# Pacing the first 24 loads of a transformer-block kernel by the landings of earlier loads

## Chip, cores and metric

The kernel runs on one core of one Trainium2 chip. The metric is device time in microseconds (us): the median of several executions. A profile's "span" is from the first to the last instruction of the profiled execution and is about 2 us shorter than the device time. Runs are compared only where they are of the same state ("fast"). A run is called slow when it is over 1.5% above the fastest run of the same kernel.

## The reference

A diffusion-transformer block with 2 batches of 256 tokens, width D = 1152, 2 heads and an MLP of 4608, in bf16. `c` gives six modulation vectors.

```python
mod = (silu(c) @ w_mod).reshape(B, 6, 1, D)      # w_mod: D x 6D
shift_a, scale_a, gate_a, shift_m, scale_m, gate_m = ...
h   = layernorm(x) * (1 + scale_a) + shift_a
q, k, v = split(h @ wqkv)                        # wqkv: D x 3D
a   = softmax(q k^T * Dh**-0.5) v @ wo
x   = x + gate_a * a
h2  = layernorm(x) * (1 + scale_m) + shift_m
out = x + gate_m * (gelu(h2 @ w_fc1) @ w_fc2)
```

The weights are 50 MB. Each byte is read once, so the kernel is a race between 50 MB of loads and the matmuls.

## The kernel before

All large loads go through one helper, on SyncE's queue, in program order. Each load has a completion semaphore. SyncE waits only where a load overwrites a buffer that is still in use.

```python
def dma(dst, src, nbytes, name, is_out=False, eng="sp", run=4096):
    eff = 1.0 if run >= 4096 else (1.08 if run >= 2304 else (1.15 if run >= 1536 else (1.3 if run >= 1024 else 1.42)))
    return S.op(eng, 500.0 if eng == "sp" else 150.0, lambda e: e.dma_start(dst, src), reads=[src], writes=[dst],
                name=name, dma_bytes=nbytes * eff, is_out=is_out)
```

`dma_bytes` is weighted: among these loads, those in short runs count up to 1.3 times their bytes. The first loads are issued in this order; I number them from 1:

```python
for b in range(2): dma(X[...], xv[b], ..., "ld_x%d" % b)                     # 1-2, 576 KB each
for (ka, kb) in ((0, KC), (KC, KT)):                                        # KC = 5, KT = 9
    for k0 in range(0, KT, 3): dma(WSC[...], wmod_v[...], ...)              # 3-5: 480 KB; 11-13: 384 KB (scale_a)
    for kt in range(ka, kb):   dma(WK[:, kt, :], wqkv_v[:, kt, D:2 * D], ..) # 6-10 and 14-17: 288 KB (K weights)
for k0 in range(0, KT, 3):     dma(WSH[...], wmod_v[:, k0:k0 + 3, 0:D], ...)  # 18-20: 864 KB (shift_a)
# ... cut ...
for kt in range(KT): dma(WQ[:, kt, :], wqkv_v[:, kt, 0:D], ...)              # 21-29: 288 KB; reuses WSC's space
dma(WV, ...)                                                               # 2592 KB
for k0 in range(0, KT, 3): dma(WMODR[:, k0:k0 + 3, :], wmod_v[:, k0:k0 + 3, 2 * D:6 * D], ...)  # 3 x 3456 KB
dma(WO, ...)                                                               # 2592 KB, then w_fc1, w_fc2
```

PE's order, as far as it matters: dummy matmuls to warm up; the three parts of the first w_mod product (`sca`, 128x2 outputs, loads 3 to 5), between transposes of the normalized x; K weight by weight; the second scale product; the shift product; Q; attention with V; then `rows()`, the row-modulation product of `c` with 4608 columns of w_mod. Its last third needs the third 3456 KB load, called **the last large w_mod load** from here on. Then come Wo and the MLP.

Of the kernel before, what the change touches and what calls it, by code (L numbers as in the profile page):

```python
# [544 lines left out]
def build_kernel(nc, x, c, wqkv, wo, w_mod, w_fc1, w_fc2, out):  # L545
    S = Sched()
# [4 lines left out]
    with (  # L551
# [104 lines left out]
        wfc1_v = w_fc1.rearrange("(k p) f -> p k f", p=P)  # L656
        wfc2_v = w_fc2.rearrange("(k p) f -> p k f", p=P)

        def dma(dst, src, nbytes, name, is_out=False, eng="sp", run=4096):
            eff = 1.0 if run >= 4096 else (1.08 if run >= 2304 else (1.15 if run >= 1536 else (1.3 if run >= 1024 else 1.42)))  # L660
            return S.op(eng, 500.0 if eng == "sp" else 150.0, lambda e: e.dma_start(dst, src), reads=[src], writes=[dst],  # L661
                        name=name, dma_bytes=nbytes * eff, is_out=is_out)

        def dve(cost, fn, reads, writes, name):
            return S.op("dve", cost, fn, reads=reads, writes=writes, name=name)
# [18 lines left out]


        dma(CSB[0:18, :], c.rearrange("b (k p) -> (b k) p", p=P), 18 * 256, "ld_c", eng="act")
        for b in range(2):
            dma(X[:, 2 * b:2 * b + 2, :], xv[b], 2 * P * D * 2, "ld_x%d" % b)
        for (ka, kb) in ((0, KC), (KC, KT)):
            w = (kb - ka) * P  # L690
            for k0 in range(0, KT, 3):
                dma(WSC[:, k0:k0 + 3, ka * P:kb * P], wmod_v[:, k0:k0 + 3, D + ka * P:D + kb * P], 3 * P * w * 2,
                    "ld_sc%d_%d" % (ka, k0), run=w * 2)
            for kt in range(ka, kb):
                dma(WK[:, kt, :], wqkv_v[:, kt, D:2 * D], P * D * 2, "ld_wk%d" % kt, run=2304)
# [3 lines left out]
        def wfc1_load(q):  # L699
# [5 lines left out]
             reads=[ONES], writes=[IDENT], name="ident")  # L705
# [176 lines left out]
        for kt in range(KT):  # L882
            for b in range(2):
                src, dst = HK[:, kt, b * 256:(b + 1) * 256], HX[:, kt, b * 256:(b + 1) * 256]
# [271 lines left out]
def bass_standalone__dit_block__diffusion_kernel(  # L1156
    nc: bass.Bass,
    x: bass.AP,
    c: bass.AP,
    wqkv: bass.AP,  # L1160
    wo: bass.AP,
    w_mod: bass.AP,
    w_fc1: bass.AP,
    w_fc2: bass.AP,
    out: bass.AP,
):
    build_kernel(nc, x, c, wqkv, wo, w_mod, w_fc1, w_fc2, out)
# [28 lines left out]
```

## Time and profile before

| | before |
|---|---|
| device time, median | 250.9 us (249.12 to 251.25) |
| span of the profile | 246.9 us |
| PE busy | 240.9 us, 98% |
| third part of the first w_mod product: load landed, PE began | 10.55, 10.59 us |
| first K weight landed, PE began K | 11.50, 11.90 us |
| last large w_mod load landed, PE needed it | 68.71, 69.90 us |

From the profile page of the kernel before: the head line, busy time by engine, and of the 40 equal slices (6.2 us each) PE, the granted TensorE clock, the DMA engines' busy share, all in tenths, and the bytes moved.

```profile
span 246.9 us, 4129 instructions
PE 240.9 (98%) x1814; PEld 149.5 (61%) x1823; DVE 69.9 (28%) x179; ACT 63.8 (26%) x129; POOL 19.6 (8%) x33
...
PE   7799999999999999999999999999999999999995
...
PEclk9999999999999999999999999999999999999999
DMA  6999999999999999999944560000000000000000
GB/s 245 348 378 393 391 315 411 420 425 424 408 387 341 310 365 391 393 390 383 357 137 158 191 191 3 0 0 0 3 16 16 16 19 16 16 19 16 22 28 18
```

PE never pauses after the second slice, and DMA is saturated for half of the span. The chain of waits that ended last, in order of time (start us, us, what), shows where the two meet: one load at the start, and PE alone from then on.

```profile
2.70 7.85 DMA arena<-in_w_mod_dram
10.55 0.05 issue
10.59 0.67 PE psum L680 x15
...
11.90 1.92 PE psum L680 x16
```

The table of stretches, before (columns: stretch; length; PE, weight loads, VectorE, ScalarE, GpSimd with instruction counts; granted clock, DMA share, GB/s):

```profile
0.00:12.00 12.00, 9.21 (x81) 4.62 (x82) 6.68 (x22) 7.47 (x12) 3.17 (x11) 1.00 0.84 294
12.00:24.00 12.00, 12.00 (x145) 10.63 (x145) 4.84 (x18) 2.29 (x5) 0.00 (x0) 1.00 1.06 385
24.00:36.00 12.00, 11.92 (x154) 9.19 (x153) 5.39 (x17) 5.37 (x11) 0.00 (x0) 1.00 0.99 351
36.00:48.00 12.00, 11.95 (x58) 5.66 (x58) 2.22 (x4) 1.87 (x4) 0.00 (x0) 1.00 1.04 414
```

SyncE's own waits before contain no load (the only DMA wait, of 1.1 us, is for an output store at the very end):

```profile
SPq L661 <- PE psum L680: 109.2, 21, 23.1
SPq L661 <- DVE arena L1140: 96.4, 13, 37.7
SPq L485 <- DMA out_dram<-arena: 1.1, 1, 1.1
```

So it issues loads far ahead: load 5 waits 7.85 us from issue to landing, mostly in the queue behind others.

### The profile page before, as it was taken

To read this page: it belongs to the slowest core of one execution; us is meant where nothing else is said; L and a number is where in the kernel's file an instruction comes from. 1 tells how busy PE (TensorE), PEld (TensorE's weight loads), DVE (VectorE), ACT (ScalarE), POOL (GpSimd) and SP (SyncE) were. 2 spreads that over 40 slices of the span, in tenths; PEclk is the share of its full clock that TensorE was granted. 3 is DMA by queue.
4 is the path that set the end of the run, shared out by engine and by line. 5 is a ranking of instruction groups with operands and counts; after the bars stand their busy time and mean duration, and the time that the engine had idled before them with its cause. 6 is when DMAs were issued, how large, how long until landed. Compare 5 with 4: busy or idle time off the path is not lost.

```text
span 246.9 us, 4129 instructions
## 1 busy us (share of the span) xinstructions
PE 240.9 (98%) x1814; PEld 149.5 (61%) x1823; DVE 69.9 (28%) x179; ACT 63.8 (26%) x129; POOL 19.6 (8%) x33
## 2 busy tenths in 40 slices
PE   7799999999999999999999999999999999999995
PEld 2589954566656766798544444444566666666675
DVE  3742440555322678950000000000011222211112
ACT  5630340344301404984233222333000000000000
POOL 1300000000012167500000000000000000000000
PEclk9999999999999999999999999999999999999999
DMA  6999999999999999999944560000000000000000
GB/s 245 348 378 393 391 315 411 420 425 424 408 387 341 310 365 391 393 390 383 357 137 158 191 191 3 0 0 0 3 16 16 16 19 16 16 19 16 22 28 18
DMA packets 27644, 51.59 MB, mean 209 GB/s; under 512 B 1511, under 2 KB 15591, under 8 KB 26475
## 3 DMA queue, kind: packets, MB, share of 16 engines
q1 hardware_dynamic: 27216, 50.14, 56.1%
q0 software_dynamic: 384, 1.19, 1.5%
q8 instruction: 14, 0.23, 0.4%
q14 instruction: 3, 0.02, 0.0%
q10 hardware_dynamic: 27, 0.00, 0.0%
HBM read 50.14 MB, written 1.19 MB: 208 GB/s over the span
## 4 chain that ended last, share of the span: by engine, by line
PE 93%; DMA 3%; ACT 1%; SPq 1%; issue 0%; DVE 0%
PE psum L680 91%; DMA arena<-in_w_mod_dram 3%; PE psum L683 2%; ACT arena L1049 1%; SPq L661 1%; ACT arena L1033 1%; DVE arena L785 0%; DVE arena L1139 0%; DVE arena L1140 0%; DVE arena L776 0%
## 5 line engine op out<-in xcount | busy, mean ns | idle before, releaser
L680 PE MATMUL psum<-arena 128*128 128x384 bf16 (+7 forms) x1707 | 237.1, 305 | 3.3 <-POOL arena L703 1.4
L680 PEld LDWEIGHTS psum<-arena 128*128 128x128 bf16 (+1 forms) x1716 | 143.7, 97 | 92.0 <-issue 3.9
L1139 DVE TENSOR_TENSOR arena<-psum,arena 128x384 f32<-128x384 f32 (+3 forms) x14 | 7.0, 501 | 119.1 <-PE psum L680 119.1
L1059 ACT ACTIVATE arena<-psum 128x512 bf16<-128x512 f32 (+1 forms) x44 | 22.5, 522 | 42.6 <-PE psum L680 42.6
L675 ACT ACTIVATE arena<-psum 128x512 bf16<-128x512 f32 (+7 forms) x29 | 15.4, 553 | 36.2 <-PE psum L680 33.8
L677 DVE CAST arena<-psum 128x512 bf16<-128x512 f32 (+4 forms) x23 | 14.0, 621 | 32.1 <-PE psum L680 32.0
L1028 POOL TENSOR_TENSOR arena<-arena 128x384 f32<-128x384 f32 x12 | 10.9, 912 | 11.1 <-DVE arena L1027 9.9
L724 DVE BATCH_NORM_STATS2 arena<-arena 128x6 f32<-128x384 f32 (+1 forms) x18 | 9.5, 548 | 1.1 <-DMA arena<-in_x_dram 1.0
L683 PEld LDWEIGHTS psum<-arena 128*128 128x128 bf16 (+2 forms) x107 | 6.4, 97 | 2.6 <-DMA arena<-in_c_dram 0.8
L683 PE MATMUL psum<-arena 128*128 128x128 bf16 (+2 forms) x107 | 7.8, 209 | 0.1
L1033 ACT ACTIVATE arena<-arena 128x1152 bf16<-128x1152 f32 x4 | 5.4, 1353 | 9.5 <-DVE arena L1032 9.5
L1027 DVE TENSOR_TENSOR arena<-psum,arena 128x384 f32<-128x384 f32 x12 | 6.6, 548 | 3.2 <-PE psum L680 3.0
L1140 DVE TENSOR_TENSOR arena<-arena 128x384 bf16<-128x384 f32 (+3 forms) x14 | 7.0, 501 | 0.5
L1049 ACT ACTIVATE arena<-psum,arena 128x128 bf16<-128x128 bf16 x16 | 6.1, 460 | 3.2 <-PE psum L683 2.5
L661 POOL DMA_DIRECT2D dit_scratch<-arena x2 | 1.3, 629 | 61.6 <-DVE arena L677 61.6
L1046 DVE TENSOR_SCALAR arena<-psum,arena 128x128 bf16<-128x128 bf16 x20 | 5.5, 336 | 2.0 <-PE psum L683 1.8
L924 ACT ACTIVATE arena<-psum,arena 128x256 bf16<-128x256 f32 x8 | 3.7, 470 | 6.9 <-PE psum L680 5.4
L728 POOL TENSOR_TENSOR arena<-arena 128x1 f32<-128x1 f32 x6 | 3.3, 552 | 8.3 <-DVE arena L727 8.3
L887 ACT ACTIVATE arena<-arena 128x256 bf16<-128x256 bf16 x6 | 2.5, 495 | 4.3 <-DVE arena L881 4.3
L920 DVE TENSOR_REDUCE arena<-psum 128x2 f32<-128x512 f32 x4 | 2.8, 689 | 1.5 <-PE psum L680 1.5
L785 DVE TENSOR_SCALAR arena<-psum,arena 128x256 bf16<-128x256 bf16 x7 | 2.4, 349 | 2.7 <-PE psum L683 1.4
L928 DVE TENSOR_TENSOR arena<-arena 128x512 bf16<-128x512 bf16 x4 | 2.8, 688 | 0.1
(37 smaller groups left out, 30.9 us busy)
## 6 DMA issues: line engine op xcount, KB each, us to landing
arena<-in_w_mod_dram SPq DMA_DIRECT2D x3, 3456.0 KB, 26.3
arena<-in_w_fc_dram SPq DMA_DIRECT2D x9, 1152.0 KB, 7.9
arena<-in_w_fc_dram SPq DMA_DIRECT2D x4, 2592.0 KB, 20.4
arena<-in_wqkv_dram SPq DMA_DIRECT2D x18, 288.0 KB, 10.4
arena<-in_w_mod_dram SPq DMA_DIRECT2D x3, 864.0 KB, 12.1
arena<-in_wqkv_dram SPq DMA_DIRECT2D x1, 2592.0 KB, 10.2
arena<-in_wo_dram SPq DMA_DIRECT2D x1, 2592.0 KB, 39.7
arena<-in_w_mod_dram SPq DMA_DIRECT2D x3, 480.0 KB, 7.1
```

The source lines that it names most:

```text
L675: act(c_act(n), lambda e: e.activation(out=dst, in_=src, func=ACTF.Copy), [src], [dst], name)
L677: dve(c_dve_psum16(n) if psum16 else c_dve_psum32(n), lambda e: e.tensor_copy(dst, src), [src], [dst], name)
L680: S.instr(lambda e: e.matmul(o, lhsT=l, rhs=r, start=st, stop=sp, **kw), reads=[l, r], writes=[o])
L683: S.instr(lambda e: e.transpose(o, i_, idn), reads=[i_, idn], writes=[o])
L724: dve(550, lambda e, s=s, o=o: e.bn_stats(out=o, in_=s), [s], [o], "bn_%s_%d" % (tag, ci))
L1027: dve(550, lambda e, o=o, ga=ga, x1c=x1c: e.tensor_tensor(out=x1c, in0=o, in1=ga, op=ALU.mult), [o, ga], [x1c], "wo_t1_%d_%d" % (t, ci))
L1028: S.op("pool", 930, lambda e, xs=xs, x1c=x1c: e.tensor_tensor(out=x1c, in0=x1c, in1=xs, op=ALU.add), reads=[x1c, xs], writes=[x1c], name=" ...
L1033: act(1344, lambda e: e.activation(out=xn2, in_=x1, func=ACTF.Identity, scale=rs, bias=nm), [x1, rs, nm], [xn2], "xn2_%d" % t)
L1049: act(440, lambda e, o=o, dst=dst, s1=s1, s2=s2: e.activation(out=dst, in_=o, func=ACTF.Identity, scale=s1, bias=s2), [o, s1, s2], [dst], ...
L1059: act(c_act(ntok), lambda e: e.activation(out=dst, in_=o, func=ACTF.Gelu_apprx_tanh), [o], [dst], "gelu_%d_%d" % (f, tok0))
L1139: dve(c_dve_psum32(w), lambda e, o=o, gm=gm, t1=t1: e.tensor_tensor(out=t1, in0=o, in1=gm, op=ALU.mult), [o, gm], [t1], "fc2_t1_%d_%d" % ( ...
L1140: dve(c_dve_32(w), lambda e, t1=t1, x1c=x1c, ost=ost: e.tensor_tensor(out=ost, in0=t1, in1=x1c, op=ALU.add), [t1, x1c], [ost], "fc2_out_%d ...
```

## The change

The intent: no load should compete with an earlier one that PE needs sooner. Each of the first 24 loads waits until the load about 1.2 MB (weighted) ahead of it has landed. Nothing else changes; the order of instructions on every engine is the same.

```diff
+        flight = []
+
         def dma(dst, src, nbytes, name, is_out=False, eng="sp", run=4096):
             eff = ...
-            return S.op(eng, ...)
+            u = S.op(eng, ...)
+            if eng == "sp" and not is_out and len(flight) < 24:
+                ahead = 0
+                for v in reversed(flight):
+                    ahead += v.dma_bytes
+                    if ahead > 1.2e6:
+                        u.instrs[0].deps.add(v.instrs[0])
+                        break
+                flight.append(u)
+            return u
```

More of the change, by code (lines that the diff above doesn't have):

```diff
@@ L657, in build_kernel @@
         wfc2_v = w_fc2.rearrange("(k p) f -> p k f", p=P)
+        flight = []
         def dma(dst, src, nbytes, name, is_out=False, eng="sp", run=4096):
             eff = 1.0 if run >= 4096 else (1.08 if run >= 2304 else (1.15 if run >= 1536 else (1.3 if run >= 1024 else 1.42)))
-            return S.op(eng, 500.0 if eng == "sp" else 150.0, lambda e: e.dma_start(dst, src), reads=[src], writes=[dst],
-                        name=name, dma_bytes=nbytes * eff, is_out=is_out)
+            u = S.op(eng, 500.0 if eng == "sp" else 150.0, lambda e: e.dma_start(dst, src), reads=[src], writes=[dst],
+                     name=name, dma_bytes=nbytes * eff, is_out=is_out)
+            if eng == "sp" and not is_out and len(flight) < 24:
[7 more added lines that the diff above has]
+            return u
         def dve(cost, fn, reads, writes, name):
```

## The prediction

> **What bounds the kernel now.** The page: PE 98% busy in a span of 246.9 us, and the chain of waits is PE for 93%. The only other large piece is a DMA wait of 7.85 us at the start: the third of the first three w_mod loads, issued at 2.70, landed at 10.55 us. PE idles 0.6 us for it and 0.8 us for the VectorE step behind it (timeline). After 11.9 us PE has no gap over 0.25 us. So better loading gains only in the first 12 us: VectorE is busy with layernorm until 10.57 us and did that step at 11.29, so at most about 0.7 us (0.3%).
>
> **What the change does.** The order of instructions is the same on all engines; SyncE alone gets waits on landings among the first 24 loads. Intended: no later load competes with the one PE needs next. There is little to win: by 9.75 us the DMA engines had moved about 2.66 MB, and x plus the three w_mod loads are 2.65 MB.
>
> **What it costs.** An isolated load (the last three w_fc1 loads, 1152 KB) takes 5.6 us from issue to landing; its packets (1024 bytes, 46 ns each on 16 engines) take 3.3 us of it: about 2.3 us fixed, my estimate. [...] A paced load has this covered only if about 0.7 to 0.85 MB are still queued when its wait ends. The rule leaves less in places (estimates):
> - second w_mod load: 0.49 MB left, bubble 0.7 us
> - first K weight: 0.5 us; two or three others 0.1 to 0.25 us
> - second Q weight: it waits for the last shift load with one 0.29 MB load behind that: 1.3 us.
>
> Total about 2.6 us of lost DMA time.
>
> **What lies on the critical path.** (a) The third w_mod load lands 0.3 to 0.5 us later (about 11.0), and PE's K stage with it. (b) The DMA queue is backlogged from 2 to 69 us, so lost time is not recovered. The last large w_mod load (4608 columns) lands at 68.71 and PE needs it at 69.9: 1.2 us of slack. Landing 2.6 us later, it stalls PE in the row-modulation stage: total shift 2.6 - 1.2 = 1.4 us, which contains (a). Loads after it have more slack (Wo 8.7 us, first w_fc1 24 us).
>
> **Prediction.** 250.9 + 1.4 = 252.3 us; range 250.3 to 254.3. Faster by over 2%: 0.005; within 2%: 0.965; slower by over 2%: 0.03.
>
> **What would show it.** SyncE's waits gain rows ending with DMA landings. GB/s falls in the first two slices and near 30 us. The third w_mod load lands near 11.0 us. SyncE issues the Q weights at 28 to 35 us, not 19 to 25. The chain of waits shows a DMA piece from in_w_mod near 70 us, about 1 us long. PE busy time and granted clock stay.
>
> **What would make it wrong.** A load alone may be quicker (less queueing): then the bubbles halve and the effect is under 0.5 us. If different DMA engines are slow at different times, pacing adds up the slowest of each load: a loss of 4 us, 253.5. If PE idles longer before 12 us its clock may drop (the skill's "TensorE: Matmul & The Clock Gate", Part 1, gives a window of about 3.4 us; this trace has the first 5.7 us of matmuls at half rate, 427 ns for 512 columns): 1.5 us more.

## The result, and the profile after

The changed kernel took 260.02 us in the median of 4 fast runs (257.56 to 260.88) against 250.95 us. The ratio is 1.0376, with a 95% interval of 1.0309 to 1.0444: slower. (The ratios are taken from fast runs alone; they are not quite the ratios of the medians, which here would give 1.0361.) The predicted 252.3 us, with its range of 250.3 to 254.3, was wrong.

The profile page, after, the same lines:

```profile
span 255.5 us, 4140 instructions
PE 243.7 (95%) x1823; PEld 150.6 (59%) x1823; DVE 69.9 (27%) x179; ACT 63.8 (25%) x129; POOL 19.6 (8%) x33
...
PE   6679999999987999999999999999999999999995
...
PEclk9959999999999999999999999999999999999999
DMA  6798969999999999999995334000000000000000
GB/s 246 227 293 248 302 203 345 406 425 420 421 419 389 353 368 363 393 392 378 392 332 182 105 111 169 0 0 0 0 18 15 15 18 15 15 18 15 15 29 21
```

Slices 2 to 6 of the GB/s line lost between a fifth and over a third. The clock fell to half in the third slice, and PE has a new gap in slices 12 and 13. The chain after:

```profile
1.23 4.62 DMA arena<-in_x_dram
5.84 0.02 issue
5.86 4.33 DMA arena<-in_w_mod_dram
10.18 0.02 issue
10.20 3.98 DMA arena<-in_wqkv_dram
14.18 0.14 issue
14.31 3.57 PE psum L691 x16
...
36.33 4.32 DMA arena<-in_wqkv_dram
...
44.90 33.52 DMA arena<-in_w_mod_dram
78.42 0.04 issue
78.47 6.13 PE psum L691 x63
```

Loads now hang on loads: x, a w_mod part, a K weight, each issued at the landing of another. The last large w_mod load lands at 78.42 us (68.71 before), and PE starts on it at 78.47. From there on PE waits for no load. 78.47 - 69.90 = 8.57 us, and the spans differ by 255.5 - 246.9 = 8.6 us: the whole loss has arisen by that point.

SyncE's waits after, where the loads have come in:

```profile
SPq L663 <- DMA arena<-in_w_mod_dram: 9.0, 6, 2.1
SPq L663 <- DMA arena<-in_wqkv_dram: 8.3, 6, 4.2
SPq L474 <- DMA arena<-in_w_mod_dram: 5.9, 2, 4.2
SPq L663 <- DMA arena<-in_x_dram: 3.7, 1, 3.7
```

The table of stretches after:

```profile
0.00:12.00 12.00, 7.90 (x65) 3.76 (x65) 6.01 (x19) 7.47 (x12) 3.17 (x11) 1.00 0.72 230
12.00:24.00 12.00, 10.23 (x103) 8.15 (x104) 3.69 (x11) 2.29 (x5) 0.00 (x0) 0.72 0.88 273
24.00:36.00 12.00, 12.00 (x165) 10.95 (x163) 4.59 (x13) 2.39 (x4) 0.00 (x0) 1.00 0.83 274
36.00:48.00 12.00, 11.61 (x87) 5.63 (x84) 2.62 (x13) 2.98 (x7) 0.00 (x0) 1.00 0.92 327
```

The last column times 12 us gives the bytes by 48 us: (294 + 385 + 351 + 414) x 12 = 17.3 MB before, (230 + 273 + 274 + 327) x 12 = 13.2 MB after. The missing 4.1 MB, at the 414 GB/s of the last stretch before, are 9.9 us of DMA time. The landings say the same: load 24 (the fourth Q weight) landed 42.07 - 32.31 = 9.8 us later, and the last large w_mod load 9.7 us later. Nothing of the loss is recovered on the way, and none is added after load 24.

How the lateness grew, from the trace's record of landings (us):

| load | before | after | late by |
|---|---|---|---|
| 5, third w_mod part | 10.55 | 11.98 | 1.4 |
| 6, first K weight | 11.50 | 14.18 | 2.7 |
| 10, fifth K weight | 14.86 | 17.36 | 2.5 |
| 13, last of the second w_mod part | 18.12 | 21.78 | 3.7 |
| 17, last K weight | 21.52 | 27.36 | 5.8 |
| 20, last shift load | 29.30 | 36.27 | 7.0 |
| 24, fourth Q weight | 32.31 | 42.07 | 9.8 |
| last large w_mod load | 68.71 | 78.42 | 9.7 |

### The profile page after: what moved, and what is told of

The parts are those of the page before. It is cut to its first block, busy times and chain, and to the rows that moved or that the text cites. A ratio compares the mean times of both kernels' runs of the same rounds, so it can differ in the third digit from the quotient of the medians.

```text
span 255.5 us, 4140 instructions
## 1 busy us (share of the span) xinstructions
PE 243.7 (95%) x1823; PEld 150.6 (59%) x1823; DVE 69.9 (27%) x179; ACT 63.8 (25%) x129; POOL 19.6 (8%) x33
## 4 chain that ended last, share of the span: by engine, by line
PE 76%; DMA 20%; SPq 2%; ACT 1%; issue 0%; DVE 0%
PE psum L691 74%; DMA arena<-in_w_mod_dram 15%; DMA arena<-in_wqkv_dram 3%; DMA arena<-in_x_dram 2%; SPq L663 2%; PE psum L694 2%; ACT arena L1060 1%; ACT arena L1044 1%; DVE arena L1150 0%; DVE arena L1151 0%
## 5 line engine op out<-in xcount | busy, mean ns | idle before, releaser
L1039 POOL TENSOR_TENSOR arena<-arena 128x384 f32<-128x384 f32 x12 | 10.9, 912 | 11.1 <-DVE arena L1038 10.0
L794 ACT ACTIVATE arena<-psum,arena 128x256 bf16<-128x256 bf16 x3 | 1.3, 472 | 9.7 <-PE psum L691 6.5
```

The source lines that it names most:

```text
L1039: S.op("pool", 930, lambda e, xs=xs, x1c=x1c: e.tensor_tensor(out=x1c, in0=x1c, in1=xs, op=ALU.add), reads=[x1c, xs], writes=[x1c], name=" ...
```

## The experiments

All outputs are right. The theories:

- **A.** What counts is the DMA time lost by load 24. It passes unchanged to the last large w_mod load, and the 1.2 us of slack there are subtracted. Whatever PE loses before it only shortens its wait for it.
- **B.** PE's separate stalls add up, each a loss by itself.
- **C.** The early part (late K, clock at half) is the cause.

On why so much DMA time was lost: the **simple model** of the prediction (one server with a fixed cost per load), and **S**: a landing is that of the slowest of 16 DMA engines, and the fast ones run dry meanwhile. The Trainium skill ("DMA: Bandwidth & Descriptors", "Why a DMA increments its semaphore by 16 and not by 1") says that a DMA runs on up to 16 engines that finish independently. The trace agrees: in the changed kernel the 16 increments of one of the first 24 loads lie 0.5 to 2.6 us apart. Pacing is not what spreads them: in the kernel before it is 0.4 to 2.8 us, and in e11, which loses nothing, 0.6 to 2.9. There the DMA share stayed at 0.99 to 1.06 from 12 to 36 us (before), so the fast engines were not idle but went on with later loads.

e1 to e8 ran on one chip, e9 to e12 on another.

### e1: only the late part paced

```diff
-                    if ahead > 1.2e6:
+                    if ahead > 1.2e6 and len(flight) >= 10:
```

> Loads 1 to 10 (x, first w_mod, K weights 0 to 4) are free, only loads 11 to 24 are paced. In the changed kernel the landings ran late against before by 2.5 us after load 10 and by 9.7 us at load 24, and the last 4608-column w_mod load landed 9.7 us late against 1.2 us of slack. Theory A (what counts is the DMA time lost before that load, less its slack): about 9.7 - 2.5 = 7.2 us late there, so the kernel is 7.2 - 1.2 = 6.0 us slower than before, with the clock at full speed and K starting near 11.9 us. Rival B (PE's stalls add up: 4.9 us early, 0.7 and 3.0 us later): taking the early pacing away takes away the 4.9 us, so 3.7 us slower. Rival C (what costs is the cold TensorE clock and the late K stage): under 1 us slower.

Measured: 256.93 us median of 4. Two runs (256.53, 253.43) are fast, two (257.33, 258.57) slow, at clocks of 0.98 to 0.99 in all four. The ratio of the fast ones is 1.0198 (1.0092 to 1.0304), so 5.0 us, with two runs only. C is out: the late part alone costs most of the loss. A and B are both within the interval. In its profile (a slow run, so only for the order of events) PE began on the last large w_mod load at 76.96 us, at that load's landing of 76.92. Here, after a stall of about 3 us at that load, the clock record shows half speed from 77.7 to 81.1 us, which lengthens this run after the load as well.

### e2: only the early part paced

```diff
-            if eng == "sp" and not is_out and len(flight) < 24:
+            if eng == "sp" and not is_out and len(flight) < 10:
```

> Only loads 1 to 10 are paced. PE's start of K is late as in the changed kernel (K began at 14.3 instead of 11.9 us, and half the clock until about 19.7), about 4.9 us by the second part of the w_mod product. Theory A: DMA is only about 2.5 us late at the last 4608-column w_mod load, and PE comes to it 4.9 us late, so no stall there: 4.9 us slower than before, all of it before 24 us. Rival C (early part is everything): 8 to 9 us slower. Rival B: 4.9 us. So with e1: A has 6.0 + 4.9 more than the 8.6 us of the whole, B has 3.7 + 4.9 = 8.6.

Measured: 252.93 us against 249.79; ratio 1.0123 (1.0067 to 1.018), 3.1 us, less than the 4.9 expected. In its profile the last large w_mod load landed 3.7 us late at 72.44, PE came to it at 73.47, and there was no stall, as A says; the 3.6 us by which PE was late is the loss. K began at 14.25 us, as in the changed kernel, but the clock came back sooner (0.993 over the span against 0.986).

Added up, e1 and e2 lose 8.1 us, where B expected 8.6 and A 10.9. So this sum does not speak for A, but with two fast runs in e1 it decides nothing either. What separates A from B is e6 and the table at the end.

### e3: 1.8 MB ahead

```diff
-                    if ahead > 1.2e6:
+                    if ahead > 1.8e6:
```

> The same pacing with 1.8 MB in place of 1.2 MB ahead. Simple model of the prediction (a wait ends a fixed 2.3 us before the new load's data can be complete, and what is queued behind covers it): at least 0.98 MB are queued at every wait, 2.5 us of transfer, so no bubbles: within 0.3% of before. Rival S (a landing is that of the slowest of 16 DMA engines, 1 to 2.4 us behind the first in the changed kernel, and fast engines run dry meanwhile, so 3 to 4 us of queue are needed): DMA still 2 to 4 us late at the last 4608-column w_mod load, so 1 to 3 us slower than before.

Measured: 253.78 us; ratio 1.0156 (1.0091 to 1.0221), 3.9 us slower than before. The simple model falls: the last large w_mod load landed at 74.25, 5.5 us late. The expectation overlooked three waits with only 0.88 MB queued behind them (the last shift load, the first and the fourth Q weight), but even that is 2.3 us of transfer, as long as the fixed cost; and the first K weight, with 0.98 MB queued, landed 2.28 us after the load before it (10.53 and 12.81 us), where its transfer takes 0.74 and the kernel before shows 0.95. The last K weight, with 1.28 MB queued, added another 1.25 us of lateness. Its stretches:

```profile
0.00:12.00 12.00, 8.11 (x80) 4.17 (x80) 6.70 (x22) 7.47 (x12) 3.17 (x11) 0.99 0.82 272
12.00:24.00 12.00, 11.06 (x111) 8.89 (x112) 3.20 (x11) 2.29 (x5) 0.00 (x0) 0.73 0.98 324
24.00:36.00 12.00, 12.00 (x172) 10.89 (x171) 4.38 (x12) 2.39 (x4) 0.00 (x0) 1.00 0.84 279
36.00:48.00 12.00, 12.00 (x57) 5.40 (x56) 2.62 (x13) 2.98 (x7) 0.00 (x0) 1.00 1.02 372
```

By 48 us it had moved 15.0 MB, 2.4 MB less than before. S expected 2 to 4 us of DMA time lost and a time 1 to 3 us slower: right in kind, too small.

### e4 and e11: 2.4 MB ahead

```diff
-                    if ahead > 1.2e6:
+                    if ahead > 2.4e6:
```

> The same pacing with 2.4 MB ahead. Both the simple model and rival S (slowest engine; 1.5 MB or more, about 4 us of queue, are left at each wait) expect DMA never to run dry: within 0.5% of before, perhaps 0.1 to 0.3% faster if keeping later loads back helps the third w_mod load (lands at 10.55 us before). If waiting for landings costs something in itself, whatever the depth, it stays 1% or more slower.

> One more look at 2.4 MB, since the profile of e4 fell in a slow state (TensorE at 0.75 of its clock all through). Expected: loads 1 to 24 landed by 35 to 36 us as in before, no stall at the last 4608-column w_mod load, span 247 to 249 us.

Measured in e4: fast runs 251.17, 250.81 and 249.28; ratio 1.0016 (0.9947 to 1.0085), the same as before. Its profiled run fell in a state with the clock at 0.754 throughout (319.25 us), so its times are not used; but its load 24 landed at 31.54 us, not later than before (32.31). e11 looked again: 249.10 us in one run (so its state is unknown), span 247.1, clock 1.0. Its stretches:

```profile
0.00:12.00 12.00, 9.05 (x80) 4.48 (x80) 6.54 (x22) 7.47 (x12) 3.17 (x11) 1.00 0.85 307
12.00:24.00 12.00, 11.95 (x144) 10.60 (x145) 4.99 (x18) 2.29 (x5) 0.00 (x0) 1.00 1.06 380
24.00:36.00 12.00, 12.00 (x156) 9.24 (x154) 5.38 (x17) 5.25 (x11) 0.00 (x0) 1.00 0.98 341
36.00:48.00 12.00, 12.00 (x59) 5.59 (x58) 2.06 (x4) 1.82 (x5) 0.00 (x0) 1.00 1.03 413
```

17.3 MB by 48 us, as before. So waiting for landings costs nothing in itself; the depth decides. The gain that the change was after is not there either: load 5 landed at 10.70 us (10.55 before).

### e5: the changed kernel again

> The changed kernel once more, so that the next two can be set against it on one chip: 3.8% (8 to 10 us) slower than before.

258.70 us, one of the four runs (261.23) being slow; ratio 1.0382 (1.0308 to 1.0456). The last large w_mod load landed at 77.92, span 255.0.

### e6: the clock kept up

```diff
+        warm(3, "c")
         for kt in range(3, 6):
             mod_kt(WSC, kt, 0, "sca_%d" % kt, (0, KC))
+        warm(6, "d")
         for kt in range(6, 9):
             mod_kt(WSC, kt, 0, "sca_%d" % kt, (0, KC))
+        warm(8, "e")
```

> The changed kernel with 17 dummy matmuls (3 before the second, 6 before the third part of the first w_mod product, 8 between it and K) so that PE does not idle and the TensorE clock stays up while K waits. In the changed kernel the clock fell to half from about 12.7 to 19.7 us, which cost PE about 2.5 us. Theory A (the last 4608-column w_mod load sets the time; what PE loses before it only shortens the wait for it): clock near 1.0, PE about 2.5 us earlier until 70 us, then the stall at that load 2.5 us longer; time as in the changed kernel within 1 us. Rival B (stalls add up): 2.5 us faster than the changed kernel. Rival C (the cold clock and late K are the cause): most of the 9 us back.

Measured: 258.00 us; ratio 1.0319 (1.0273 to 1.0366). The mean of the fast runs is 257.98 us, that of e5's 258.14: no gain. The clock did stay at 1.00 until 24 us, and PE reached the shift product earlier (32.83 us against 33.69 in e5). There it waited for the second and third shift loads (1.0 and 1.4 us), the clock fell there instead (0.73 from 36 to 48 us), and it came to the last large w_mod load just before it landed, at 78.31. From its chain of waits:

```profile
45.04 33.27 DMA arena<-in_w_mod_dram
78.31 0.04 issue
78.36 6.13 PE psum L691 x63
```

A holds, B (2.5 us faster) and C fall. The detail that A had wrong is where the waiting moved to: mostly to the shift loads. The drop of the clock was moved and not removed (mean 0.987 in both profiles), so e6 clears the early drop alone; e10, where it is removed, follows below.

### e7 and its control e9: more slack at the load

e7 is the changed kernel, e9 the kernel before, both with two V products put ahead of the row-modulation product (and the transposes of its result, `rows_T`, one V product later):

```diff
         v_proj(2, 0)
+        v_proj(2, 1)
+        v_proj(2, 2)
         rows()
         wfc1_load(0)
         wfc1_load(1)
-        v_proj(2, 1)
-        v_proj(2, 2)
         v_proj(3, 0)
-        rows_T()
         v_proj(3, 1)
+        rows_T()
```

> The changed kernel, with the product that needs the last 4608-column w_mod load put two V products (2.9 us) later in PE's order. Theory A: the load has 2.9 us more slack, the stall of 3.0 us at it all but goes, and the kernel is 2.5 to 3 us faster than the changed one, so 5.5 to 6 us slower than before. If that load's lateness is not what sets the time, no change. A risk: the gates that come of this product arrive later and stall the Wo part, which would eat up some of the gain.

> Control for e7: the same move of two V products ahead of the row-modulation product in the kernel before, which has 1.2 us of slack at that load and no stall there. Expected: within 0.5% of before (the later gates may cost up to 1 us in the Wo part). If the move itself gains 1 us or more, e7's gain was not the stall at the load.

Measured in e7: 256.15 us; ratio 1.0254 (1.0202 to 1.0307). The mean of its runs is 256.36 us, 1.8 us below e5's fast runs, less than expected. In e9: 252.22 us; ratio 1.0082 (1.0027 to 1.0137), outside the expected 0.5%. Some of that is clock: three of its four runs were at 0.993. Among runs of equal clock the move costs 1.4 us (spans 250.2 to 250.4 against 248.3 to 249.3 at 0.993; 248.6 against 247.2 at 1.0), in new waits for the gates in the Wo part. Taking that off, the extra slack was worth about 1.8 + 1.4 = 3.2 us, of the size that A expected. This is a difference of small numbers on two chips, so it supports A but does not prove it. In e7's profile, of the slowest of its runs, the load landed at 80.32 us, 1.9 us later than in the changed kernel, and PE began on it at 80.36; yet the span, 255.3 us, is no longer.

### e8: one load at a time

```diff
-                    if ahead > 1.2e6:
+                    if ahead > 0:
```

> Each of the first 24 loads waits for the landing of the one before it. This measures the disputed cost by itself. Prediction's figure: 2.3 us fixed for each load beside its transfer: a 288 KB K or Q weight 3.05 us from issue to landing, a 480 KB w_mod load 3.6 us, an 864 KB shift load 4.5 us, with the 16 engines finishing within about 0.5 us of each other. If so, the fixed cost was sized right and the shortfall is in what overlap does (dry engines, spread); if the small loads take 4 us and over, the fixed cost itself was too small. Kernel about 50 us slower than before; time is not the point here.

300.52 us in one run. This is the fixed cost by itself. Two lines of the profile's list of DMA issues, of the stretch from 19 to 54 us, where each load was alone (the last column is the median us from issue to landing):

```profile
arena<-in_wqkv_dram SPq DMA_DIRECT2D x9, 288.0 KB, 2.8
arena<-in_w_mod_dram SPq DMA_DIRECT2D x3, 384.0 KB, 3.3
```

A 2304-byte packet takes 93 ns in the stream, and a K weight is 8 of them on each engine, 0.74 us; so about 2.1 us are fixed. The last two shift loads took 4.5 and 4.6 us, 2.3 to 2.4 of it fixed (the first took 6.0). All but three of the first 24 loads had their 16 increments within 0.3 to 0.8 us (the three: 1.0, 1.4 and 1.9). The fixed cost of the prediction (2.3 us) lies within what these loads show, 2.1 to 2.4. It is not all a wait for the first byte: of the nine K weights, the first packet starts 0.97 us after the issue and the last one ends 2.4 to 2.6 us after it. Of their 1152 packets 118 took over 200 ns, all of them among the first 56 of a load's 128 to start.

### e10: early part paced, clock kept up

The edit is e2's and e6's together.

> Early pacing alone (e2, 3 us slower than before) with the 17 dummy matmuls of e6. In e2 PE came to the last 4608-column w_mod load 3.6 us late, and the load was 3.7 us late with 1.2 us of slack, so it allowed 2.5 us. Theory A: the clock stays up, PE gains 1 to 2 us before 70 us, and the load's landing then holds the gain to about 1.1 us: 2 to 2.5 us slower than before. Stalls adding up (B): the whole cold-clock loss of about 1.7 us comes back, 1.3 us slower than before.

Measured: 252.26 us; ratio 1.0102 (1.0059 to 1.0145), 2.5 us, in A's range but for another reason: PE came to the last large w_mod load at 73.25, after its landing at 72.44, so the landing held nothing. The clock was 1.0 in all four runs, but the loads came later still (the fifth K weight at 19.31 against 18.20 in e2), and PE waited for them. It decides nothing between A and B.

### e12: dummies in the kernel before

```diff
+        warm(3, "d")
         for kt in range(6, 9):
             mod_kt(WSC, kt, 0, "sca_%d" % kt, (0, KC))
+        warm(3, "e")
```

> The kernel before with 3 dummy matmuls ahead of the third part of the first w_mod product and 3 ahead of K, into its two gaps of 0.75 and 0.9 us. About half of the runs of before have a granted clock of 0.993 and are 1.7 us longer than those at 1.000. If the gaps let the clock fall there, the dummies keep it at 1.000: 0.8 us (0.3%) faster in the mean. If the clock's ramp at the start is what differs, no change.

Measured: 249.37 us over 6 runs, 249.19 to 249.94; ratio 0.9989 (0.9955 to 1.0024). All six had a clock of 0.999 or more, while of the 11 runs of before 4 were at 0.992 or 0.993 and 1 to 2 us longer. The trace of e9, at 0.993, shows what such a run is: half speed from 12.2 to 15.6 us, although PE's two early waits (0.3 and 0.8 us) are no longer than in the profiled run of before (0.6 and 0.8), which has no drop. That the dummies end the spread is likely but not shown: at 4 in 11, six clean runs in a row would come by chance about once in fifteen. The mean does not gain clearly.

### The runs side by side

Landing of the last large w_mod load, the time at which PE began on it, and the span, from the profiles (e7 and e9 have another order and e8 another scale):

| run | landed | PE began | span | PE later than before | span longer than before |
|---|---|---|---|---|---|
| before | 68.71 | 69.90 | 246.9 | | |
| e11, 2.4 MB | 68.82 | 70.06 | 247.1 | 0.2 | 0.2 |
| e10, early, warm | 72.44 | 73.25 | 250.3 | 3.4 | 3.4 |
| e2, early | 72.44 | 73.47 | 250.5 | 3.6 | 3.6 |
| e3, 1.8 MB | 74.25 | 74.30 | 251.3 | 4.4 | 4.4 |
| e5, as changed | 77.92 | 77.96 | 255.0 | 8.1 | 8.1 |
| e6, warm | 78.31 | 78.36 | 255.4 | 8.5 | 8.5 |
| changed | 78.42 | 78.47 | 255.5 | 8.6 | 8.6 |

In the last four rows PE began within 0.05 us of the landing: the load sets the time. In e2 and e10 PE itself was later than the load. PE's stall at this load was 3.0 us in the changed kernel, 1.4 in e5 and 0.4 in e6, with spans within 0.5 us of each other: the same end, reached by different roads. That is the evidence against adding stalls up.

## Why the prediction was wrong

- **What bounds the kernel, and the instruction order:** right. The most that could be gained was put at 0.7 us; at 2.4 MB ahead, where pacing costs nothing, nothing was gained.
- **The fixed cost of a load, 2.3 us:** right; e8 measured 2.1 to 2.4.
- **The step that failed: "Total about 2.6 us of lost DMA time."** It measured 9.7 us. The step before it, "A paced load has this covered only if about 0.7 to 0.85 MB are still queued when its wait ends", is the reason. By that rule e3, with 0.88 MB or more at each wait, should have lost nothing; it lost 5.5 us, 1.3 of them at a wait with 0.98 MB and as much at one with 1.28 MB. At 2.4 MB the same arithmetic leaves at least 1.47 MB, and nothing was lost. So the cover needed lies between 1.3 and 1.5 MB by the order of issue (3.3 to 3.8 us at 390 GB/s). In the changed kernel the three bubbles that the prediction named measured about 0.9 us (second w_mod load), 1.25 (first K weight) and 2.35 (second Q weight), 4.5 in place of 2.5; the other 5 us arose mostly at waits with 0.7 to 1.0 MB queued, where it saw 0.1 to 0.25 us two or three times.
- **What was missing in that arithmetic.** I treated the 16 engines as one server. Summing the trace's packets from 1.8 us to the last Q weight (33.5 us long before, 43.2 after, the same 12 MB), the mean engine had about 6.5 us more without a packet, and its packets took 3.3 us longer in total. The sum is rough, since packets overlap: before, they come to slightly more than the stretch itself. The first is what S expects: the wait ends with the slowest engine, and the others have run dry by then. (The trace does not name a packet's engine, so this was not seen directly.) The second is that packets are slow when engines start again after a pause, as in e8: of the 2304-byte packets that started before 46 us, 47 of 4608 took over 200 ns before, and 197 of 3702 after, the longest 1.4 us, against 93 ns in the stream. The two may feed each other, since a slow first packet can make a slowest engine. In the changed kernel the first K weight had 1.75 us between its first and last increment, and took 3.98 us, against 2.9 alone in e8. For a load alone, the slow packets are part of the fixed cost that e8 measured and do not come on top of it. How much each contributes was not separated: the test for it, a wait for the first of the 16 increments, was not run. Why a packet can take 1.4 us is open as well. What the runs do show is that the loss depends on the depth: 9.7 us at 1.2 MB, 5.5 at 1.8, none at 2.4.
- **"(a) The third w_mod load lands 0.3 to 0.5 us later":** it landed 1.4 us later, and K began 2.4 us later. The same term, too small.
- **"total shift 2.6 - 1.2 = 1.4 us, which contains (a)":** the form was right. With the measured term it reads 9.7 - 1.2 = 8.5 us, and the span grew by 8.6. The loss shows at the named load, as the chain piece near 70 us that the prediction asked for (it came at 78). In e5, e6 and the changed kernel the early losses are contained in it.
- **"its clock may drop":** it did, to half from 12.7 to 19.5 us, but in the full pacing this cost nothing by itself (e6).
- **"If different DMA engines are slow at different times, pacing adds up the slowest of each load":** this was the right direction of the error, but its 4 us were too few; the runs do not tell which part of it was too small.

## What to carry to other kernels

When a queue of loads is saturated from the start to a later point where PE has little slack, every microsecond of DMA idleness before that point, beyond the slack, is paid there unless PE itself is later still (e2); compare bytes moved by a given time, not stalls. If loads are to be paced by landings, the data left in flight must cover not only the fixed cost of a load but also, it seems, the spread between the DMA engines: here 1.3 to 1.5 MB, not the 0.8 MB that the fixed cost alone asks for. And this queue already gave the earlier load its turn (before, the first 34 loads landed in the order of issue): before pacing a queue, count whether bytes of later loads really went ahead of it.

## What the Trainium skill lacked or had wrong

- "DMA: Bandwidth & Descriptors", "Anatomy of one DMA": its fixed cost of about 2.0 us is measured for DMAs that GpSimd issues; the loads here, issued by SyncE, had 2.1 to 2.4 us in e8. It lacks what is lost when DMA engines run dry between loads: packets of 0.2 to 1.4 us after a pause where 93 ns is the rate in the stream, and 9.7 us lost over 24 loads that were paced about 1.2 MB apart.
- The same page, "Why a DMA increments its semaphore by 16 and not by 1": it says that the engines finish independently but not how far apart; the runs show 0.3 to 0.8 us for most loads that are alone (e8), and 0.4 to 2.8 us for loads in a full queue (before). It has no advice on how many bytes to keep in flight when loads wait for landings.
- "TensorE: Matmul & The Clock Gate", Part 1, gives about 3.4 us of idleness as what lets the clock fall. Here it fell after much shorter waits. In the changed kernel the record has half speed from 12.7 to 19.5 us: PE had waited 0.5 and 1.3 us, with bursts of 15 two-column matmuls (0.55 us) after each, and the third wait, of 1.8 us, had just begun. The K matmuls from 14.3 us on were 213 ns apart and not 109. In e9 it fell at 12.2 us after a wait of 0.3 us, in one of 0.8. That such bursts hardly count as busy is a guess; no run tests it. The timeline of the changed kernel, with the idle time before each group in brackets (the first group's wait is the 0.5 us):

```profile
10.23 0.55 PE L691 MATMUL psum<-arena 128*128 128x2 bf16 x15 [0.54 <-DMA arena<-in_w_mod_dram]
12.02 0.55 PE L691 MATMUL psum<-arena 128*128 128x2 bf16 x15 [1.25 <-DMA arena<-in_w_mod_dram]
14.31 3.57 PE L691 MATMUL psum<-arena 128*128 128x256 bf16 x16 [1.75 <-DMA arena<-in_wqkv_dram]
```
